# Moving two weight stores and two raw weight loads ahead of the first output weights' store, and stores of sums ahead of stores of weights

## The chip, the core and the metric

The kernel runs on one core of a Trainium2 chip. The time is the device time of one execution in microseconds; a result is the median of several. The engines are TensorE (PE, matrix products), VectorE (DVE), ScalarE (ACT), GpSimd (POOL) and SyncE (SP), which here does no arithmetic and only issues transfers (DMAs) between the chip's main memory (DRAM) and the on-chip memory (SBUF). ACT issues a few DMAs of its own. Each engine takes its instructions in a fixed order, and one that has to wait holds up everything behind it on that engine.

## The reference

```python
# attention in chunks of 64 positions: q, k, v are (8, 8, 576, 64)
scores = scale * np.matmul(q_c, k_c.transpose(0, 1, 2, 4, 3))
attn = np.exp(scores - np.max(scores, axis=-1, keepdims=True))
attn = attn / (np.sum(attn, axis=-1, keepdims=True) + 1e-09)
out = np.matmul(attn, v_c)
# gated feed-forward: x is (4608, 512), w_gate and w_val (512, 1536), w_out (1536, 512)
g = x @ w_gate
silu = g * (1.0 / (1.0 + np.exp(-g)))
val = x @ w_val
return (silu * val @ w_out).astype(np.float32)
```

The three weight matrices come as 64-bit floats, q, k and v as 32-bit ones.

## The kernel before

The 4608 tokens are cut into nine blocks of 512, and the 1536 hidden units into twelve groups f of 128. The first two blocks, `a0` and `a1`, go through the groups together, one step for each f, and the weights are prepared on the way; later blocks read the prepared weights back from DRAM. This case is about that opening, the first 116 us.

A product that must be close to 32-bit precision is done as three passes: each factor is split into an upper half (a rounded copy, made by ACT) and a lower half (the rest, made by DVE). One product of a block with a group's gate or value weights is 12 matmuls of 128x512.

These weights pass through the opening:

- **Raw up-weights**, `Up(f).load` (line 109): gate and value columns of group f as 64-bit words, a load of 1 MB. Below they are called raw f. ACT (`scale`, line 80, and `below`, line 87) and DVE (`shift`, line 83, and `join`, line 90) turn them into 32-bit floats `t`; `upper` (ACT, line 124) and `lower` (DVE, line 130) split those into the tile `w` of group f.
- **Stores of weights**, `save_w(f)` (line 197): the split tile w f goes to DRAM, 1 MB, for later blocks.
- **Sums**, `Quarters(f)`: DVE makes sums and differences of quarters of `t` (lines 148 to 150) in the tile `ts`; `upper` (ACT, line 162) and `lower` (DVE, line 165) split them into the tile `th`, and `save` (line 170) stores the two halves, 0.5 MB each. Below that pair of stores is t f. Through step 6 there is one `th` buffer: the halves for group f + 1 can only be written when t f has landed in DRAM.
- **Raw output weights**, `Out(f).load` (line 236): 1 MB for two groups, so only an even f issues a load (wo 2, wo 4); for an odd f it issues nothing. `out_weights(f)` (line 63 on DVE is its last part) splits them, and `save_o(f)` (line 489) stores o f, 0.5 MB.
- **put_off** (line 577): ACT issues a store of 0.25 MB in each step, the hidden values of `a1`.

One step f, for f from 1 to 5 (the loop of line 808), puts five pieces of 12 matmuls on PE: the gate of `a0`, its value, the projection of `a0` for the step before (lines 538 to 540), the gate of `a1`, its value. The products (line 475) share two PSUM buffers (`ps_gv`): a value of `a0` can start when DVE has taken the value of `a1` of the step before (`times`, line 519), a value of `a1` when DVE has taken that of `a0`, and a gate when ACT has taken the gate before it (`silu`, line 512). In between DVE and ACT prepare group f + 1, and from step 2 on they also make sums of the blocks' inputs (lines 773 to 786, tiles `sums` and `x`), which are put where w 0 to w 3 and raw 3 were. From step 6 (line 857) each product of the pair is replaced by seven smaller ones.

PE, ACT, DVE and, through the opening, SP run in the order in which the code is written (`manual_schedule`). So the order of SP's DMAs is that of the calls: in the opening's text, and then at the head of each step (lines 810 to 816) and, for f up to 2, line 823. Which buffer a tile takes is set by its tag: raw 3 lies in `w8`, where the first attention stage kept its turned exponents, wo 2 where `a0` kept its scores.

The line numbers of the profile of before are those of this listing.

Of the kernel before, what the change touches and what calls it, by code (L numbers as in the profile page):

```python
# [33 lines left out]
def attn_then_gated_ffn(ctx: ExitStack, tc: tile.TileContext, qk, v, wgv, wo, out):  # L34
# [19 lines left out]
    def keep_warm(n):  # L54

        ps = ps_gv.tile([P, P], F32, name="unread", tag="ps_gv")
        for _ in range(n):
            nc.tensor.transpose(ps, ident, ident)
# [78 lines left out]
    class Quarters:  # L137
# [12 lines left out]
            engine.tensor_tensor(out=s[:, 3], in0=t[:, 1], in1=s[:, 2], op=ALU.subtract)  # L150

        def place(self):
            if self.f >= SEVEN and self.f % 2:
                if not odd_t:
                    odd_t.extend(xs.tile([P, 4 * Q], F32R, name="th", tag=tag) for tag in ("xh0", "xl0"))
                return list(odd_t)
            both = const.tile([P, 2, 4 * Q], F32R, name="th", tag="th")
            return [both[:, 0], both[:, 1]]
# [14 lines left out]
    SEVEN, EARLY = 6, 4  # L173
# [21 lines left out]
    def save_w(f):  # L195
        kept_w[f] = store.tile([P, 2, 4 * Q], F32, name=f"w{f}")
        nc.sync.dma_start(out=kept_w[f], in_=w_both[f].bitcast(F32))
# [279 lines left out]
    def out_weights(f):  # L477
        both = wp.tile([P, 2, DM], F32R, name="both", tag="wo")
        split(wo_raw[f], both[:, 0], both[:, 1])
        if f % 2 == 0:  # L480
            o = store.tile([P, 2, 2, DM], F32, name=f"o{f}")
            kept_o[f], kept_o[f + 1], two_o[f // 2] = o[:, 0], o[:, 1], o
        out_now[f] = both
        return both[:, 0], both[:, 1]
# [3 lines left out]
    def save_o(f):  # L488
        nc.sync.dma_start(out=kept_o[f], in_=out_now[f].bitcast(F32))
# [17 lines left out]
    def gate(a, f):  # L507
        return silu(product(a, f, 0))

    def silu(pg):  # L510
        h = hp.tile([P, N], F32, name="h")
        nc.scalar.activation(h, pg, AF.Silu, scale=2.0 ** -8)
        return h

    def value(a, f):
        return product(a, f, 1)

    def times(h, pv):
        nc.vector.scalar_tensor_tensor(out=h, in0=pv, scalar=2.0 ** -8, in1=h, op0=ALU.mult, op1=ALU.mult)  # L519
# [6 lines left out]
    def parts(a, f, h):  # L526
        hh = hp.tile([P, N], F32R, name="hh")
        hl = hp.tile([P, N], F32R, name="hl")
        split(h, hh, hl)
        return a, f, hh, hl  # L530
# [27 lines left out]
    def lag(parts, wo_f):  # L558

        if pending:  # L560
            project(*pending.pop())
        if parts is not None:
            pending.append((parts, wo_f))
# [5 lines left out]
    up, down = [Up(f) for f in range(NF)], [Out(f) for f in range(NF)]  # L569
    waiting = []  # L570

    def put_off(h):
        f = len(waiting)
        if f % 2 == 0:
            kept_h.append(store.tile([P, 2, N], F32, name=f"h{f}"))
        waiting.append(kept_h[-1][:, f % 2])
        nc.scalar.dma_start(out=waiting[f], in_=h)
# [141 lines left out]
    for do in opening.split():  # L719
        if do[0] == ".":  # L720
            keep_warm(int(do[1:]))
        elif do[0] in "gvw":
            getattr(weights[do[:-1]], steps[do[-1]])()
        elif do[0] in "GV":
            if do[0] not in products:
                products[do[0]] = Product(a0, 0, "GV".index(do[0]))
            products[do[0]].add((int(do[3]), int(do[4])))
        elif do[0] == "e":
            a0.exchange(v0[int(do[1])][:, 1], values[int(do[1])][1], nc.scalar.copy)
        elif do == "H0":  # L730
            h0 = silu(products["G"].ps)
        elif do == "Q0":
            times(h0, products["V"].ps)
        else:
            b, i = int(do[1]), int(do[2])
            pairs = do[0] in "STCUL"
            getattr(couples[b, i // 2 if pairs else i], do[0])(i if pairs else int(do[3:] or 0))
    w = up[1]
    pg, pv = Product(a1, 0, 0), Product(a1, 0, 1)
    pg.add((0, 1), (1, 1), (0, 2), (1, 2), (2, 1), (3, 1), (2, 2), (3, 2))  # L740
# [5 lines left out]
    pv.add((0, 0), (1, 0), (2, 1), (3, 1), (2, 2), (3, 2), (2, 0), (3, 0))  # L746
    pv1 = pv.ps
    w.lower()
    o.shift()
    o.join()  # L750
    quarters = Quarters(1)
# [1 line left out]
    p0 = parts(a0, 0, h0)  # L753
    wo_f = out_weights(0)
    lag(p0, wo_f)
    down[1].load()
    down[1].scale()
    quarters.upper()

# [47 lines left out]

    for f in range(1, SEVEN):
        w, o = up[f + 1], down[f]
        save_o(f - 1)  # L810
        up[f + 2].load()
        if f <= EARLY:
            save_w(f - 1)
        if f > 2:
            quarters.save()
        down[f + 1].load()
        ahead.get(f, lambda: None)()
        h0 = gate(a0, f)
        times(h1, pv1)
        put_off(h1)  # L820
        if f <= 2:
            quarters.lower()
            quarters.save()
        quarters = Quarters(f + 1)
        w.shift()
        w.below()
        pv0 = value(a0, f)
        o.shift()
        o.below()
        beside.get(f, lambda: None)()  # L830
        w.join()
        w.upper()
        times(h0, pv0)
        within.get(f, lambda: None)()
        p0 = parts(a0, f, h0)
        w.lower()
        o.join()
        quarters.sums(w.t)
        up[f + 2].scale()
        wo_f = out_weights(f)  # L840
        lag(p0, wo_f)
        h1 = gate(a1, f)
        quarters.upper()
        down[f + 1].scale()
        if f > 1:
            quarters.lower()
        pv1 = value(a1, f)
# [402 lines left out]
    for i in range(NF):  # L1250
        f = (i + EARLY) % NF
# [67 lines left out]
```

## Time and profile before

| | us |
|---|---|
| median of 3 runs | 904.18 (902.27 to 905.06) |
| the profiled execution | 903.28 |
| its span | 901.5 |
| PE busy in the span | 885.2 (98%) |
| DVE busy | 545.6 (61%) |
| ACT busy | 386.1 (43%) |

The span runs from the first to the last recorded instruction; the remaining 1.78 us of the execution lie around it. A row of the timeline reads: start in the span, length, engine, line and operation, what it writes and from what, the shape, how many, and in square brackets how long the engine stood idle before it and what ended that. "SPq" and "ACTq" are issues of DMAs; the length there is that of the issue, not of the transfer. 223.25 MB are moved in all, at a mean of 248 GB/s. The granted clock of TensorE is 1.00 throughout.

### The profile page before, as it was taken

To read this page: it belongs to the slowest core of one execution; us is meant where nothing else is said; L and a number is where in the kernel's file an instruction comes from. 1 tells how busy PE (TensorE), PEld (TensorE's weight loads), DVE (VectorE), ACT (ScalarE), POOL (GpSimd) and SP (SyncE) were. 2 spreads that over 40 slices of the span, in tenths; PEclk is the share of its full clock that TensorE was granted. 3 is DMA by queue.
4 is the path that set the end of the run, shared out by engine and by line. 5 is a ranking of instruction groups with operands and counts; after the bars stand their busy time and mean duration, and the time that the engine had idled before them with its cause. 6 is when DMAs were issued, how large, how long until landed. Compare 5 with 4: busy or idle time off the path is not lost.

```text
span 901.5 us, 14751 instructions
## 1 busy us (share of the span) xinstructions
PE 885.2 (98%) x6047; PEld 731.7 (81%) x6047; DVE 545.6 (61%) x834; ACT 386.1 (43%) x587; POOL 17.1 (2%) x18
## 2 busy tenths in 40 slices
PE   7998999999999999999999999999999999999998
PEld 6776788878888888888888888888888888888886
DVE  5869899853787655775763646776645533333332
ACT  4846677653514335324233445234334432223232
POOL 1200000000021000000000000000000000000000
PEclk9999999999999999999999999999999999999999
DMA  9297977799898657755586857665667565556651
GB/s 358 112 377 264 323 291 274 291 315 349 271 359 286 253 198 258 258 213 180 217 294 236 333 185 282 233 228 195 220 245 242 212 237 201 196 220 233 234 187 47
DMA packets 73170, 223.25 MB, mean 248 GB/s; under 512 B 30736, under 2 KB 30992, under 8 KB 58896
## 3 DMA queue, kind: packets, MB, share of 16 engines
q1 hardware_dynamic: 71664, 219.70, 67.3%
q10 hardware_dynamic: 1440, 2.62, 0.8%
q8 instruction: 47, 0.77, 0.3%
q14 instruction: 19, 0.16, 0.0%
HBM read 178.78 MB, written 43.52 MB: 247 GB/s over the span
## 4 chain that ended last, share of the span: by engine, by line
PE 90%; DMA 4%; DVE 4%; ACT 1%; issue 1%; POOL 0%; SPq 0%; ACTq 0%
PE ps_a L857 25%; PE ps_gv L857 19%; PE ps_o L538 11%; PE ps_o L539 10%; PE ps_o L540 10%; PE ps_gv L475 10%; DMA t<-th 3%; PE ps_a L287 2%; PE ps_a L365 1%; DMA qk_t<-in_qk 1%; ACT th L162 0%; DVE sums L776 0%; PE ps_a L451 0%; PE ps_a L465 0%; DVE th L165 0%
## 5 line engine op out<-in xcount | busy, mean ns | idle before, releaser
L857 PE MATMUL ps_a<-x,factors 128*128 128x512 f32 x864 | 219.3, 389 | 0.0
L857 PEld LDWEIGHTS ps_a<-x,factors 128*128 128x128 f32 x864 | 162.2, 188 | 33.7
L857 PE MATMUL ps_gv<-x,factors 128*128 128x512 f32 x648 | 164.5, 389 | 0.0
L857 PEld LDWEIGHTS ps_gv<-x,factors 128*128 128x128 f32 x648 | 121.7, 188 | 25.2
L538 PE MATMUL ps_o<-both,hl 128*128 128x512 f32 x336 | 132.3, 394 | 0.2 <-DVE hl L63 0.2
L539 PE MATMUL ps_o<-both,hh 128*128 128x512 f32 x336 | 131.0, 390 | 0.0
L540 PE MATMUL ps_o<-both,hh 128*128 128x512 f32 x336 | 130.9, 389 | 0.0
L475 PE MATMUL ps_gv<-xh,w 128*128 128x512 f32 x384 | 117.0, 390 | 0.2 <-ACT xh L614 0.2
L63 DVE TENSOR_TENSOR hl<-h,hh 128x512 fp32r<-128x512 f32 x98 | 67.6, 690 | 61.7 <-ACT hh L62 61.5
L62 ACT CAST hh<-h 128x512 fp32r<-128x512 f32 x98 | 60.4, 617 | 96.1 <-PE ps_o L540 51.3
L861 DVE TENSOR_TENSOR h<-h,ps_gv 128x512 f32<-128x512 f32 x42 | 28.8, 686 | 105.6 <-PE ps_gv L857 105.4
L352 DVE STREAM_TRANSPOSE turned<-s_sb 32x256 f32<-32x256 f32 x192 | 83.7, 436 | 2.7
L475 PEld LDWEIGHTS ps_gv<-xh,w 128*128 128x128 f32 x384 | 72.0, 188 | 15.7 <-issue 0.7
L519 DVE SCALAR_TENSOR_TENSOR h<-v,h 128x512 f32<-128x512 f32 x84 | 58.1, 692 | 37.7 <-ACT h L1153 33.0
L475 PE MATMUL ps_gv<-xl,w 128*128 128x512 f32 x192 | 74.0, 395 | 5.3 <-DVE h L519 2.9
L538 PEld LDWEIGHTS ps_o<-both,hl 128*128 128x128 f32 x336 | 63.1, 188 | 14.1 <-DVE hl L63 0.7
L540 PEld LDWEIGHTS ps_o<-both,hh 128*128 128x128 f32 x336 | 63.1, 188 | 13.2
L539 PEld LDWEIGHTS ps_o<-both,hh 128*128 128x128 f32 x336 | 63.1, 188 | 12.7
L1153 ACT ACTIVATE h<-ps_a 128x512 f32<-128x512 f32 x36 | 21.5, 599 | 112.2 <-PE ps_a L857 112.2
L861 DVE TENSOR_TENSOR v<-v,ps_a 128x512 f32<-128x512 f32 x42 | 28.8, 687 | 41.1 <-PE ps_a L857 36.4
L475 PEld LDWEIGHTS ps_gv<-xl,w 128*128 128x128 f32 x192 | 36.0, 188 | 14.2 <-DVE h L519 4.5
L1139 ACT ACTIVATE h<-h 128x512 f32<-128x512 f32 x36 | 22.8, 632 | 53.0 <-DVE h L861 52.9
(132 smaller groups left out, 1007.4 us busy)
## 6 DMA issues: line engine op xcount, KB each, us to landing
factors<-w SPq DMA_DIRECT2D x36, 1024.0 KB, 4.8
factors<-t SPq DMA_DIRECT2D x36, 1024.0 KB, 6.0
both<-o SPq DMA_DIRECT2D x70, 512.0 KB, 6.3
w<-w SPq DMA_DIRECT2D x16, 1024.0 KB, 9.7
t<-th SPq DMA_DIRECT2D x24, 512.0 KB, 5.8
two<-o SPq DMA_DIRECT2D x12, 1024.0 KB, 5.0
raw<-in_wgv SPq DMA_DIRECT2D x11, 1024.0 KB, 8.2
qk_t<-in_qk SPq DMA_DIRECT2D x10, 1024.0 KB, 8.4
```

The lines of the kernel that those rows point to most:

```text
L62: nc.scalar.copy(out=hi, in_=src)
L63: (engine or nc.vector).tensor_tensor(out=lo, in0=src, in1=hi.bitcast(F32), op=ALU.subtract)
L352: nc.vector.transpose(out=self.turned[to:to + 32, p:p + 2, j, :, 32 * (i % 2):32 * (i % 2) + 32], in_=src[32 * i:32 * i + 32, :, o // 2, 3 ...
L475: nc.tensor.matmul(ps, w, x, start=first and (k, i) == which[0], stop=last and (k, i) == which[-1])
L519: nc.vector.scalar_tensor_tensor(out=h, in0=pv, scalar=2.0 ** -8, in1=h, op0=ALU.mult, op1=ALU.mult)
L538: nc.tensor.matmul(o, hl[:, ts], woh, start=f == a.steps[0], stop=False)
L539: nc.tensor.matmul(o, hh[:, ts], wol, start=False, stop=False)
L540: nc.tensor.matmul(o, hh[:, ts], woh, start=False, stop=f == a.steps[1])
L857: nc.tensor.matmul(ps, w[u][:, k], x[i][v][:, k], start=first and k == 0 and n == 0, stop=k == NK // 2 - 1 and n == 2, skip_group_check=True)
L861: nc.vector.tensor_tensor(out=t, in0=t, in1=ps, op=ALU.add)
L1139: nc.scalar.activation(h, h, AF.Silu, scale=2.0 ** -8)
L1153: nc.scalar.activation(h2, ps1, AF.Silu, scale=2.0 ** -8)
```

## The change

No instruction is added or removed on any engine: SP has 310 rows in the order of both versions, and PE, DVE, ACT and POOL run the same instructions in the same order. What moves is SP's DMAs.

```diff
@@ class Quarters
         def place(self):
-            if self.f >= SEVEN and self.f % 2:
+            if (self.f - SEVEN) % 2 and self.f > SEVEN:
@@ after the opening's list of steps
+    save_w(0)
+    up[3].load()
+    down[1].load()
+    down[2].load()
     w = up[1]
...
     w.lower()
+    save_w(1)
     o.shift()
...
     lag(p0, wo_f)
-    down[1].load()
     down[1].scale()
@@ the loop over steps
     for f in range(1, SEVEN):
         w, o = up[f + 1], down[f]
+        if f > 1:
+            up[f + 2].load()
         save_o(f - 1)
-        up[f + 2].load()
-        if f <= EARLY:
-            save_w(f - 1)
         if f > 2:
             quarters.save()
-        down[f + 1].load()
+            if f <= EARLY:
+                save_w(f - 1)
+        if f > 1:
+            down[f + 1].load()
         ahead.get(f, lambda: None)()
```

`SEVEN` is 6 and `EARLY` is 4. The new condition in `place` picks the same groups as the old one (7, 9 and 11).

The first place is SP's queue from the end of the opening's loads to the stores of step 2. `raw<-in_wgv` is a raw up-weight (raw 3, then raw 4), `raw<-in_wo` the raw output weights (the first row wo 0, the second wo 2), `w_` a store of weights (w 0, then w 1), `o_` a store of output weights (o 0, then o 1), `t_` the two stores of sums (t 1, then t 2). Before:

```order
L236 DMA raw<-in_wo 128x2x512
L489 DMA o_707<-both 128x1024
L109 DMA raw<-in_wgv 128x1024
L197 DMA w_716<-w 128x2048
L236 DMA raw<-in_wo 128x2x512
L170 DMA t_739<-th 128x1024 x2
L489 DMA o_707<-both 128x1024
L109 DMA raw<-in_wgv 128x1024
L197 DMA w_830<-w 128x2048
L170 DMA t_850<-th 128x1024 x2
```

and after the change:

```order
L236 DMA raw<-in_wo 128x2x512
L197 DMA w_661<-w 128x2048
L109 DMA raw<-in_wgv 128x1024
L236 DMA raw<-in_wo 128x2x512
L197 DMA w_700<-w 128x2048
L489 DMA o_715<-both 128x1024
L170 DMA t_741<-th 128x1024 x2
L109 DMA raw<-in_wgv 128x1024
L489 DMA o_715<-both 128x1024
L170 DMA t_850<-th 128x1024 x2
```

w 0, raw 3, wo 2 and w 1 now stand ahead of o 0, behind which all of them stood; between o 0 and t 1 nothing is left, where raw 3, w 0 and wo 2 were; raw 4 now stands ahead of o 1.

The second place is SP's queue in steps 3 and 4, from step 3's first row on (raw 5, o 2, w 2, t 3, wo 4, then raw 6, o 3, w 3, t 4 are what is issued). Before:

```order
L489 DMA o_894<-both 128x1024
L109 DMA raw<-in_wgv 128x1024
L197 DMA w_944<-w 128x2048
L170 DMA t_946<-th 128x1024 x2
L236 DMA raw<-in_wo 128x2x512
L489 DMA o_894<-both 128x1024
L109 DMA raw<-in_wgv 128x1024
L197 DMA w_1060<-w 128x2048
L170 DMA t_1062<-th 128x1024 x2
```

and after the change:

```order
L109 DMA raw<-in_wgv 128x1024
L489 DMA o_894<-both 128x1024
L170 DMA t_944<-th 128x1024 x2
L197 DMA w_947<-w 128x2048
L236 DMA raw<-in_wo 128x2x512
L109 DMA raw<-in_wgv 128x1024
L489 DMA o_894<-both 128x1024
L170 DMA t_1060<-th 128x1024 x2
L197 DMA w_1063<-w 128x2048
```

Each step's raw load now stands ahead of its store of output weights, and each store of sums ahead of the store of weights.

## The prediction

> **What bounds the kernel now.** PE is busy for 885.2 of 901.5 us, so only its gaps can be won. I first read PE's waits, then its timeline from 44 to 120 us, the only stretch in which SP's order changes and PE still has gaps. The waits, with their total, count and longest:
>
> ```profile
> PE ps_gv L475 <- DVE h L519: 2.9, 4, 1.2
> PE ps_gv L475 <- ACT h L512: 1.7, 1, 1.7
> ```
>
> The timeline places all five, and gives PE's pace:
>
> ```profile
> 47.83 0.39 PE L538 MATMUL ps_o<-both,hl 128*128 128x512 f32 x1
> ...
> 58.25 0.62 PE L475 MATMUL ps_gv<-xh,w 128*128 128x512 f32 x2
> ...
> 61.42 0.39 PE L538 MATMUL ps_o<-both,hl 128*128 128x512 f32 x1
> ...
> 68.19 0.50 PE L475 MATMUL ps_gv<-xl,w 128*128 128x512 f32 x1 [1.17 <-DVE h L519]
> ...
> 72.87 0.50 PE L475 MATMUL ps_gv<-xl,w 128*128 128x512 f32 x1 [1.66 <-ACT h L512]
> ...
> 75.27 0.61 PE L475 MATMUL ps_gv<-xh,w 128*128 128x512 f32 x2
> 76.17 0.50 PE L475 MATMUL ps_gv<-xl,w 128*128 128x512 f32 x1 [0.29 <-DVE h L519]
> ...
> 90.31 0.50 PE L475 MATMUL ps_gv<-xl,w 128*128 128x512 f32 x1 [0.23 <-DVE h L519]
> ...
> 105.37 0.50 PE L475 MATMUL ps_gv<-xl,w 128*128 128x512 f32 x1 [1.17 <-DVE h L519]
> ...
> 116.39 0.39 PE L857 MATMUL ps_a<-xl,w 128*128 128x512 f32 x1
> ```
>
> From 47.83 to 61.42, without a gap, 60 matmuls take 13.59 us, 0.2265 each. From 61.42 to step 6 there are 216 more, 48.92 us: step 6 would begin at 110.34, and begins at 116.39. So the five gaps cost **6.05 us**: 4.52 recorded, and some 0.3 each for emptying and refilling the array (the first matmul takes 0.50 instead of 0.39). That is the ceiling.
>
> Why are DVE and ACT late there? ACT's timeline answers:
>
> ```profile
> 60.88 1.05 ACT L162 CAST th<-ts 128x1024 fp32r<-128x1024 f32 x1 [6.47 <-DMA t<-th]
> ...
> 62.89 1.14 ACT L87 ACTIVATE t<-raw 128x1024 int32<-128x1024 uint32 x1
> ...
> 72.22 0.59 ACT L512 ACTIVATE h<-ps_gv 128x512 f32<-128x512 f32 x1
> ...
> 75.98 0.60 ACT L512 ACTIVATE h<-ps_gv 128x512 f32<-128x512 f32 x1 [0.20 <-PE ps_gv L475]
> ...
> 76.52 1.16 ACT L87 ACTIVATE t<-raw 128x1024 int32<-128x1024 uint32 x1
> ...
> 102.41 1.05 ACT L162 CAST th<-ts 128x1024 fp32r<-128x1024 f32 x1 [2.95 <-DMA t<-th]
> ```
>
> Twice ACT waits for the store of sums to leave `th`, and DVE waits behind it. DVE's rows that PE's gaps hang on:
>
> ```profile
> 64.05 2.36 DVE L773 TENSOR_TENSOR sums<-xh,xl 128x1024 f32<-128x1024 f32 x2
> ...
> 67.45 0.69 DVE L519 SCALAR_TENSOR_TENSOR h<-ps_gv,h 128x512 f32<-128x512 f32 x1
> ...
> 75.44 0.68 DVE L519 SCALAR_TENSOR_TENSOR h<-ps_gv,h 128x512 f32<-128x512 f32 x1
> ...
> 89.57 0.68 DVE L519 SCALAR_TENSOR_TENSOR h<-ps_gv,h 128x512 f32<-128x512 f32 x1
> ...
> 104.64 0.68 DVE L519 SCALAR_TENSOR_TENSOR h<-ps_gv,h 128x512 f32<-128x512 f32 x1
> ```
>
> **The first wait.** The five issues from o 0 to t 1 (first and last row), and the landing of t 1's halves from SP's line 170:
>
> ```profile
> 44.33 0.34 SPq L489 DMA_DIRECT2D o<-both  x1
> ...
> 46.53 1.38 SPq L170 DMA_DIRECT2D t<-th  x2
> ```
>
> ```profile
> DMA to landing us min/median/max: 12.1/12.9/13.7
> ```
>
> o 0, raw 3, w 0, wo 2 and t 1 are 4.5 MB (0.5 and four of 1), done at 60.88, 16.55 us after the first issue: 3.7 us per MB. With the change, w 0 issues after its lower half, raw 3 and wo 2 when PE has read the old content, w 1 after its lower half:
>
> ```profile
> 35.78 0.86 PE L465 MATMUL ps_a<-pT,v_t 64*64 64x64 f32 x43
> ```
>
> ```profile
> 24.70 0.77 DVE L222 TENSOR_TENSOR w<-t,w 128x512 fp32r<-128x512 f32 x1
> ...
> 39.18 1.22 DVE L130 TENSOR_TENSOR w<-t,w 128x1024 fp32r<-128x1024 f32 x1
> ...
> 44.81 1.22 DVE L165 TENSOR_TENSOR th<-ts,th 128x1024 fp32r<-128x1024 f32 x1
> ```
>
> That is 25.5, 36.7 and 40.4 us, in a stretch where the queues are empty:
>
> ```profile
> 36.00:44.00 8.00, 7.84 (x75) 6.47 (x65) 7.35 (x13) 6.87 (x12) 0.00 (x0) 1.00 0.01 3
> ```
>
> (the last two numbers are the DMA engines' share and GB/s). raw 3, wo 2 and w 1, 3 MB from 36.7, are through at 47.8; o 0 and t 1, 1.5 MB more, at 53.4. ACT wanted `th` from 60.88 - 6.47 = 54.41. The wait goes, with 1 us to spare, and 3 more before it would be felt, as now follows.
>
> **What is late next.** The 6.5 us don't all arrive. ACT's `below` (62.89) stands behind the silu of `a0`'s gate, which waits for PE: in step 3 the gate's last pair ends at 75.88, and `below` starts at 76.52, 0.64 later. In step 2 the pair ends at 58.87, so `below` starts at 59.51, **3.38 us** earlier. The sums at 64.05 wait for its end, and what follows on DVE and ACT up to 76 us moves by the same 3.38, since both then run with waits for each other alone. Against PE's ungapped times (61.42 plus 24, 36, 48 matmuls, then 13.59 a step):
>
> - 68.19: the value of `a1` is due at 66.86; `times` at 67.45 comes at 64.07. Gone.
> - 72.87: the gate is due at 69.57; the silu at 72.22 comes at 68.84 and frees the buffer 0.65 later, at 69.49. Gone, by 0.1 us.
> - 76.17: due at 72.29; `times` at 75.44 comes at 72.06 and PE starts 0.73 later, 72.79. Stays, 0.50 late, and 0.12 for the slower first matmul.
> - 90.31: DVE needs 14.13 us from one `times` (75.44) to the next (89.57), more than PE's 13.59. It comes at 86.19, PE at 86.93 against a due 86.50. Stays; PE is now 86.93 + 0.12 - 85.88 = 1.17 behind the ungapped time.
> - 105.37: without the second wait `th` is written at 102.41 - 2.95 - 3.38 = 96.08, and `times`, 2.23 behind that, at 98.31; done at 99.0, PE wants it at 100.64. Gone, with 1.6 us to spare.
>
> Sum: 6.05 - 1.17 = **4.9 us**.
>
> **The second wait.** It takes t 4 landing by 96.08. SP's rows, and the landings of t 3 and wo 4 (lines 170 and 236):
>
> ```profile
> 73.76 0.32 SPq L489 DMA_DIRECT2D o<-both  x1
> ...
> 75.42 1.40 SPq L170 DMA_DIRECT2D t<-th  x2
> 78.27 0.38 SPq L236 DMA_DIRECT2D raw<-in_wo  x1
> ...
> 89.59 1.04 SPq L170 DMA_DIRECT2D t<-th  x2
> ```
>
> ```profile
> DMA to landing us min/median/max: 10.8/11.0/11.1
> ```
>
> ```profile
> DMA to landing us min/median/max: 11.0/11.0/11.0
> ```
>
> From o 2 (73.76) to t 4 (landed by 102.4, where ACT's wait ends) nine SP entries are 8 MB, plus two of ACT's 0.25: 28.6 us for 8.5 MB. The change takes raw 5 out ahead (it issues after t 2) and puts w 3 behind: 6.5 MB, 21.9 us from an o 2 that comes at 73.76 - 3.38 = 70.4: landed at 92.3, 3.8 us early. That counts on transfers finishing in the queue's order, as here: t 3, issued at 75.42 and about 76, is in by 87; wo 4 behind it at 89.3.
>
> The Trainium skill's page "DMA: Bandwidth & Descriptors" (Queues, rings and completion order) says that descriptors are consumed in ring order but completion is not in order of issue. Were t 4 to share the engines with w 3 behind it, being ahead would gain nothing; the landings above speak for ring order, and the sum goes by them. By that rule the time is the second rival's.
>
> **The rest costs nothing, for these reasons.** `place` picks the same groups. No byte is added. The early transfers run beside DVE: its 128x1024 subtraction takes 1.22 us at 39.18, with idle DMA, and 1.22 at 44.81, with busy ones; bound 0 either way. w 0's store, at 25.5, may start beside raw 2, which ACT takes without a wait at
>
> ```profile
> 30.96 1.13 ACT L80 ACTIVATE t<-raw 128x1024 f32<-128x1024 f32 x1
> ```
>
> In the queue's order that costs 0, shared at most w 0's own 3.7 us; I take 0, by the order of t 3 and wo 4. What SP's queue holds up: behind raw 3, which waits for PE until 36.7, stand wo 2, w 1, o 0 and t 1, and o 0 and t 1 are not ready before 44.3 and 46.0. Behind the raw loads of steps 2 to 5 stand the stores, but their buffers were read a step before. w 2 and w 3 go later than t: ACT writes `x` over w 2 at
>
> ```profile
> 92.89 1.04 ACT L782 CAST x<-sums 128x1024 fp32r<-128x1024 f32 x1
> ```
>
> less 3.4, 89.5; w 2 issues at about 73 and the four stores of w landed within 11.7 us:
>
> ```profile
> DMA to landing us min/median/max: 9.6/10.3/11.7
> ```
>
> so by 84.7, 4.8 us early. After step 6 PE has no gap up to 190 us, so the 4.9 us carry through to the end.
>
> **The rivals.**
>
> - All five gaps vanish, if the sums' chain in steps 2 and 3 is shorter than I copy it: 6.05, 897.2 us. Against it: 14.13 per step on DVE with one wait of half a us.
> - t 4 still lands late. If completion is shared, w 3's 1 MB (3.4 us) and raw 7's count too: 92.3 + 6.8 = 99.1, `th` 3.0 late, less the 1.6 to spare: 1.4 and the refill, gain 3.4: 899.9 us. For it: the engines' rows are full here, with 8.5 MB in 28.6 us; against it the order t 3, wo 4.
> - PE gains little: t 1 lands no earlier than 60.88 - 1, because raw 3, wo 2 and w 1 issue late. The step begins to lose at 57.4 (60.67 for the sums, less 3.3 for both halves and two shifts). Then DVE moves by 1, and the gain is near 1 to 2: 902 us.
> - Slower: w 2's store, now behind t 3, holds `x`. It decides from 16 us after its issue; 1.6 are to spare on DVE, 4.9 are won, so net loss starts at 22.5 us, and 26 us give 906.8. No store took half of 22.5.
>
> **The numbers.** The profiled execution took 903.28, its span 901.5; 903.28 - 4.9 = 898.4. It lies 0.9 below the median of the runs, 904.18, on whose scale the forecast is 899.3. I give 898.8, between them. Chances: forecast 0.57 (897.4 to 900.2), all gone 0.10, t 4 late 0.18, little gain 0.11, slower 0.04. A range from 896.7 to 901.4 leaves out little gain and slower and some spread. 0.3% is 2.7 us, about what a measurement of this kernel tells from no change; faster by more takes a time below 901.5: 0.57 + 0.10 + 0.18 less 0.03 for their tails, 0.82. Within 0.3%: 0.14. Slower: 0.04.
>
> **What would show it.** ACT's wait at line 162 for `t` gone in step 1 and step 4; `below` of step 2 at about 59.5; PE's gaps reduced to two of 0.3 to 0.4 us near 72.8 and 86.9; the first matmul of line 857 at about 111.5. It is wrong if the gaps at 68 or 72 remain (the 0.1 us), if t 4's wait stays, or if a wait for `w` appears at line 782.

## The result, and the profile after

| | before | changed |
|---|---|---|
| median of 4 runs, us | 903.98 (902.27 to 905.06) | 897.48 (897.17 to 897.97) |
| the profiled execution | 903.28 | 897.36 |
| its span | 901.5 | 895.6 |

The ratio is 0.993, with a 95% interval of 0.9913 to 0.9948: 6.5 us faster by the medians, 5.9 by the two profiled executions. The forecast gain was 4.9, taken from the profiled execution.

PE's timeline of the changed kernel holds the same three marks as before (the projections of steps 1 and 2, the first matmul of step 6). Lines from the opening on are four to six higher than before: 857 is 863, 773 is 777.

```profile
47.62 0.39 PE L538 MATMUL ps_o<-both,hl 128*128 128x512 f32 x1
...
61.22 0.39 PE L538 MATMUL ps_o<-both,hl 128*128 128x512 f32 x1
...
110.22 0.39 PE L863 MATMUL ps_a<-xl,w 128*128 128x512 f32 x1
```

From 61.22 to 110.22 are 49.00 us; the ungapped time is 48.92, and before it took 54.97. All five gaps are gone, also the two that the prediction kept: 5.97 us. PE's waits say the same. Both rows at line 475 of before, 2.9 and 1.7 us, are missing, and what is left on line 475 is

```profile
PE ps_gv L475 <- ACT s_sb L368: 0.8, 1, 0.8
...
PE ps_gv L475 <- ACT xh L614: 0.2, 1, 0.2
```

which lie outside the stretch from 44 to 110 us. ACT's writing of `th`, which waited 6.47 and 2.95 us for stores:

```profile
54.02 1.05 ACT L162 CAST th<-ts 128x1024 fp32r<-128x1024 f32 x1 [0.16 <-DMA t<-th]
...
94.66 1.04 ACT L162 CAST th<-ts 128x1024 fp32r<-128x1024 f32 x1
```

The first wait: SP's rows of the opening (w 0, raw 3, wo 2, w 1, o 0, t 1), the time to landing of t 1's halves, and the rows of DVE that follow:

```profile
25.27 0.34 SPq L197 DMA_DIRECT2D w<-w  x1
36.52 0.34 SPq L109 DMA_DIRECT2D raw<-in_wgv  x1
36.95 1.16 SPq L236 DMA_DIRECT2D raw<-in_wo  x1
40.21 0.33 SPq L197 DMA_DIRECT2D w<-w  x1
44.11 0.33 SPq L489 DMA_DIRECT2D o<-both  x1
44.52 1.63 SPq L170 DMA_DIRECT2D t<-th  x2
```

```profile
DMA to landing us min/median/max: 8.1/8.1/8.2
```

```profile
56.03 0.69 DVE L519 SCALAR_TENSOR_TENSOR h<-ps_gv,h 128x512 f32<-128x512 f32 x1 [1.84 <-ACT wo L80]
56.64 1.22 DVE L165 TENSOR_TENSOR th<-ts,th 128x1024 fp32r<-128x1024 f32 x1
```

The second wait: SP's queue in steps 3 and 4, and the time to landing of t 4's halves, first in the kernel before, then in the changed one:

```profile
69.00 0.32 SPq L489 DMA_DIRECT2D o<-both  x1
69.52 1.58 SPq L170 DMA_DIRECT2D t<-th  x2
71.16 0.62 SPq L197 DMA_DIRECT2D w<-w  x1
74.58 0.38 SPq L236 DMA_DIRECT2D raw<-in_wo  x1
75.02 1.13 SPq L109 DMA_DIRECT2D raw<-in_wgv  x1
83.19 0.33 SPq L489 DMA_DIRECT2D o<-both  x1
83.71 1.58 SPq L170 DMA_DIRECT2D t<-th  x2
```

```profile
DMA to landing us min/median/max: 11.5/11.8/12.2
```

```profile
DMA to landing us min/median/max: 3.4/3.5/3.6
```

Between raw 6 at 75.02 and o 3 at 83.19 SP issues nothing, and raw 6 lands 8.8 us after its issue, at 83.8. So t 4 finds the queue almost empty but for o 3, and lands 3.5 us after its issue instead of 11.8.

ACT's `below` in step 2, and DVE's rows in step 2 and behind it, where the prediction had put the two sums together:

```profile
59.25 1.13 ACT L87 ACTIVATE t<-raw 128x1024 int32<-128x1024 uint32 x1
```

```profile
58.71 1.22 DVE L777 TENSOR_TENSOR sums<-xh,xl 128x1024 f32<-128x1024 f32 x1
60.41 1.23 DVE L777 TENSOR_TENSOR sums<-xh,xl 128x1024 f32<-128x1024 f32 x1 [0.48 <-ACT t L87]
...
70.67 0.68 DVE L519 SCALAR_TENSOR_TENSOR h<-ps_gv,h 128x512 f32<-128x512 f32 x1
...
84.86 0.68 DVE L519 SCALAR_TENSOR_TENSOR h<-ps_gv,h 128x512 f32<-128x512 f32 x1
```

Only the second sum waits for ACT's reading of raw 3 (line 87). `times` comes at 70.67, where 72.06 was forecast.

### The profile page after: what moved, and what is told of

Same layout as the page of the kernel before. It is cut to its first block, busy times and chain, and to the rows that moved or that the text cites. A ratio compares the mean times of both kernels' runs of the same rounds, so it can differ in the third digit from the quotient of the medians.

```text
span 895.6 us, 14752 instructions
## 1 busy us (share of the span) xinstructions
PE 884.2 (99%) x6047; PEld 732.2 (82%) x6047; DVE 546.6 (61%) x834; ACT 386.6 (43%) x587; POOL 17.1 (2%) x18
## 4 chain that ended last, share of the span: by engine, by line
PE 94%; DVE 2%; DMA 2%; POOL 0%; ACT 0%; issue 0%; SPq 0%; DVEq 0%; POOLq 0%
PE ps_a L863 26%; PE ps_gv L863 19%; PE ps_gv L475 13%; PE ps_o L538 11%; PE ps_o L540 11%; PE ps_o L539 11%; PE ps_a L287 2%; DMA v_t<-in_v 2%; DVE turned L352 1%; PE ps_a L365 1%; DMA qk_t<-in_qk 1%; PE ps_a L465 0%; POOL v_t L408 0%; DVE h L519 0%; PE ps_a L451 0%
## 5 line engine op out<-in xcount | busy, mean ns | idle before, releaser
L867 DVE TENSOR_TENSOR v<-v,ps_gv 128x512 f32<-128x512 f32 x42 | 28.9, 688 | 24.5 <-PE ps_gv L863 24.2
```

What stands on the lines that cost most here:

```text
L867: nc.vector.tensor_tensor(out=t, in0=t, in1=ps, op=ALU.add)
```

## The experiments

The diffs are against the changed kernel. The column "stretch" is the time on PE from the projection of step 1 (first row at line 538) to the first matmul of step 6, 276 matmuls, 62.51 us without gaps: it leaves out the opening's start, which differs by up to 0.8 us from profile to profile. The four from "opening's part only" to "raw behind o" ran on one chip beside the kernel before (904.36), the last four on another beside the kernel before (903.53); the last of these is the changed kernel once more.

| kernel | median us | stretch, from and to | stretch | gaps in it |
|---|---|---|---|---|
| before (first profile) | 903.98 | 47.83 to 116.39 | 68.56 | 4.52 in five |
| changed (first profile) | 897.48 | 47.62 to 110.22 | 62.60 | none |
| opening's part only | 898.96 | 47.96 to 112.23 | 64.27 | 1.40 in one |
| steps' part only | 901.75 | 48.33 to 114.93 | 66.60 | 2.83 in four |
| w ahead of t | 897.67 | 47.81 to 110.41 | 62.60 | none |
| raw behind o | 898.29 | 47.73 to 110.31 | 62.58 | none |
| sums swapped | 898.90 | 48.02 to 111.73 | 63.71 | 0.54 in two |
| one more store | 897.96 | 47.90 to 110.47 | 62.57 | none |
| two more stores | 900.82 | 48.24 to 113.25 | 65.01 | 1.50 in three |
| changed, again | 897.38 | 47.52 to 110.08 | 62.56 | none |

**The opening's part alone.**

```diff
 for f in range(1, SEVEN):
-        if f > 1:
-            up[f + 2].load()
         save_o(f - 1)
+        if f > 1:
+            up[f + 2].load()
+        if 2 < f <= EARLY:
+            save_w(f - 1)
         if f > 2:
             quarters.save()
-            if f <= EARLY:
-                save_w(f - 1)
```

> Keeps the opening's part of the change (w 0, raw 3, wo 2, w 1 ahead of o 0) and puts steps 2 to 5 back to the old order (o, raw, w, t). Theory: the first wait for t stays away, so PE's gaps at 68 to 90 us stay away; t 4 again has o 3, raw 6 and w 3 ahead of it, lands some 12 us after its issue as before, and ACT waits some 2.4 us for it in step 4, which leaves one gap of 0.6 to 0.9 us on PE near 99 us: about 0.9 us over the changed kernel. Rival (the steps' part is worth nothing once the opening is emptied): no wait for t 4, and the changed kernel's time.

The rows of ACT and PE, and t 4's landing:

```profile
98.25 1.05 ACT L162 CAST th<-ts 128x1024 fp32r<-128x1024 f32 x1 [3.18 <-DMA t<-th]
```

```profile
101.22 0.50 PE L475 MATMUL ps_gv<-xl,w 128*128 128x512 f32 x1 [1.40 <-DVE h L519]
```

```profile
DMA to landing us min/median/max: 11.5/12.0/12.4
```

The theory holds: t 4 lands after 12 us as before, ACT waits, one gap is back. It is 1.40 us wide, not 0.6 to 0.9, since ACT waited 3.18 us instead of 2.4. The stretch is 1.7 us longer than the changed kernel's, the median 1.3 above that of the kernel with w ahead of t, which ran beside it and has no gap; 0.9 was expected.

**The steps' part alone.**

```diff
-    save_w(0)
-    up[3].load()
-    down[1].load()
-    down[2].load()
     w = up[1]
...
     w.lower()
-    save_w(1)
...
     lag(p0, wo_f)
+    down[1].load()
...
         save_o(f - 1)
-        if f > 2:
+        if f <= 2:
+            if f == 1:
+                up[3].load()
+            save_w(f - 1)
+            down[f + 1].load()
+        else:
             quarters.save()
             if f <= EARLY:
                 save_w(f - 1)
-        if f > 1:
             down[f + 1].load()
```

> Keeps the part of the change in the steps (raw first, t ahead of w) and puts the opening back to the old order (o 0, raw 3, w 0, wo 2, then t 1). Theory: t 1 lands at about 61 as before, ACT waits 6 us for it, and PE's gaps at 68, 73, 76 and 90 us come back, 4.6 us together; the gap at 105 us stays away. So about 4.6 us over the changed kernel, 1.4 under the one before. Rival (t 1 is not what PE's gaps hang on): most of the gain stays.

ACT, and PE with all its gaps between 44 and 110 us:

```profile
60.85 1.05 ACT L162 CAST th<-ts 128x1024 fp32r<-128x1024 f32 x1 [6.06 <-DMA t<-th]
```

```profile
68.15 0.50 PE L475 MATMUL ps_gv<-xl,w 128*128 128x512 f32 x1 [0.62 <-DVE h L519]
...
72.83 0.50 PE L475 MATMUL ps_gv<-xl,w 128*128 128x512 f32 x1 [1.66 <-ACT h L512]
...
76.13 0.50 PE L475 MATMUL ps_gv<-xl,w 128*128 128x512 f32 x1 [0.29 <-DVE h L519]
...
90.32 0.50 PE L475 MATMUL ps_gv<-xl,w 128*128 128x512 f32 x1 [0.26 <-DVE h L519]
```

The first four gaps are back, the fifth isn't. The stretch is 4.0 us longer than the changed kernel's, and the medians differ by 4.3 (by 4.1 from the kernel with w ahead of t, which ran beside it); it is 2.6 us under the kernel before on the same chip, where 1.4 was expected. So the change is two cures: the opening's part does away with the first four gaps, the steps' part with the fifth. The stretch shortens by 4.29 us with the one (68.56 - 64.27), by 1.96 with the other (68.56 - 66.60) and by 5.96 with both. The two single gains add up to 0.29 more than the gain of both. That is a balance of two differences: the first gap is 0.55 narrower here than before (0.62 against 1.17), since PE came to it 0.5 us later while `th` was written at the same time, and the gap that the opening's part leaves is 0.23 wider than before (1.40 against 1.17).

**w ahead of t again, and raw behind o again.**

```diff
         if f > 2:
-            quarters.save()
             if f <= EARLY:
                 save_w(f - 1)
+            quarters.save()
```

> The changed kernel with the store of weights put back ahead of the store of sums in steps 3 and 4; raw loads stay first. Theory: t 4 lands later by w 3's own transfer, 2.5 to 3.4 us, so some 6 to 7 us after its issue instead of 3.5, at about 91; ACT wants it at 94.7, so there is no gap and no cost. Rival (completion is shared among transfers in flight, so the place in the queue does not matter): t 4 lands 3.5 us after its issue as in the changed kernel.

```diff
-        if f > 1:
-            up[f + 2].load()
         save_o(f - 1)
+        if f > 1:
+            up[f + 2].load()
```

> The changed kernel with each raw load of steps 2 to 5 put back behind the store of output weights; stores of sums stay ahead of those of weights. Theory: raw 6 stands ahead of t 4 again, which lands 6 to 7 us after its issue; no wait on ACT, no cost. Rival (raw's place is what cured step 4): ACT waits for t 4 and PE has a gap near 99 us, 0.9 us.

t 4's landing in the one and in the other, and ACT's write of `th` in the other:

```profile
DMA to landing us min/median/max: 6.1/7.3/8.5
```

```profile
DMA to landing us min/median/max: 9.5/9.9/10.3
```

```profile
95.47 1.05 ACT L162 CAST th<-ts 128x1024 fp32r<-128x1024 f32 x1 [0.61 <-DVE both L63]
```

With w 3 ahead of it t 4 takes 7.3 us instead of 3.5: its place in the queue does matter, and the rival is refuted. Raw 6 ahead of it costs more than was expected, 9.9 instead of 6 to 7; a half issued at 85.1 that takes 10.3 us is in at 95.4, and ACT writes `th` at 95.47, 0.6 us after it was free. (The profile names line 63 on DVE as what ended that wait; that instruction writes `both`, not `th` or `ts`, so the landing is the likelier cause.) Neither costs PE a gap, nor the stretch a tenth. Each of the two orders is enough by itself; the kernel before had neither, and both transfers together made the 12 us.

**The sums swapped.** The prediction's failed step, put to the test.

```diff
     def begin():
         raw.append(Raw())
-        raw[0].whole(a1, 0, S4)
         raw[0].whole(a1, 1, S1)
+        raw[0].whole(a1, 0, S4)
```

> The changed kernel, but in step 2 DVE makes the sum that lies in raw 3's place first and the other second; nothing else differs. Theory: only the sum in raw 3's place has to wait for ACT's second reading of raw 3 (line 87, ending at 60.4); the prediction took both to wait, and was 1.2 us too late on DVE. Put first, it makes both wait, as the prediction had it: DVE comes 1.2 us later from there on, PE gets two gaps of 0.3 to 0.5 us near 72.6 and 86.8, and the time is about 1.2 us over the changed kernel. Rival (the prediction's two gaps failed for another reason, such as a faster step on DVE): no gap and the changed kernel's time.

DVE's sums and the two `times` that they delay, then PE:

```profile
60.79 2.36 DVE L777 TENSOR_TENSOR sums<-xh,xl 128x1024 f32<-128x1024 f32 x2 [1.60 <-ACT t L87]
...
72.19 0.68 DVE L519 SCALAR_TENSOR_TENSOR h<-ps_gv,h 128x512 f32<-128x512 f32 x1
...
86.37 0.68 DVE L519 SCALAR_TENSOR_TENSOR h<-ps_gv,h 128x512 f32<-128x512 f32 x1
```

```profile
72.93 0.50 PE L475 MATMUL ps_gv<-xl,w 128*128 128x512 f32 x1 [0.27 <-DVE h L519]
...
87.11 0.50 PE L475 MATMUL ps_gv<-xl,w 128*128 128x512 f32 x1 [0.27 <-DVE h L519]
```

With both sums behind ACT, the two gaps that the prediction saw are there: forecast at 72.79 and 86.93, found at 72.93 and 87.11. They are 0.27 us wide, just under the 0.3 to 0.5 expected; with some 0.3 us more for each, as in the kernel before, they make the stretch 1.15 us longer (63.71 against 62.56), as expected, and the median is 1.5 above that of the changed kernel on the same chip.

**One and two more stores ahead of t 1.** The diff is that of the second kernel; the first has `range(1)`.

```diff
     save_w(1)
+    for i in range(2):
+        spare = store.tile([P, 2, 4 * Q], F32, name=f"spare{i}")
+        nc.sync.dma_start(out=spare, in_=w_both[1].bitcast(F32))
```

> The changed kernel with one more 1 MB store (w 1 once more, to a tile that nobody reads) between w 1 and o 0. Theory: t 1 lands 2.5 to 3.7 us later, at 56.5 to 57.7 instead of 54.0; the first sum of step 2 loses its place in front of ACT's reading of raw 3, and DVE is 0.5 to 1.6 us later: 0.5 to 1.7 us over the changed kernel. Rival (3 us to spare, as predicted): no cost.

> The changed kernel with two more 1 MB stores between w 1 and o 0. Theory: t 1 lands 5 to 7.4 us later, at 59 to 61.4, ACT waits 5 to 7 us for it, and PE's gaps of the kernel before come back: 3.5 to 5.3 us over the changed kernel, with every us of t 1 beyond the first mega-byte costing about one. Rival: the gaps have another cause, and the time stays within 1 us of the changed kernel.

ACT's write of `th` in step 1, with one and with two:

```profile
55.79 1.05 ACT L162 CAST th<-ts 128x1024 fp32r<-128x1024 f32 x1 [1.59 <-DMA t<-th]
```

```profile
59.15 1.05 ACT L162 CAST th<-ts 128x1024 fp32r<-128x1024 f32 x1 [4.61 <-DMA t<-th]
```

t 1's time to landing in the changed kernel (second profile), with one and with two:

```profile
DMA to landing us min/median/max: 7.3/7.4/7.6
```

```profile
DMA to landing us min/median/max: 9.6/9.8/10.0
```

```profile
DMA to landing us min/median/max: 12.6/12.8/13.0
```

One store more costs nothing that the runs can tell: no gap, a stretch of 62.57, and 897.96 against 897.38 with overlapping ranges. That expectation missed: `th` written at 55.8 is still early enough. Two cost 2.45 us in the stretch and 3.4 in the median (just under the 3.5 to 5.3 expected), with `th` 3.4 us later than with one; of the first four gaps three are back, near 71, 74 and 89 us, and the one at 68 is not. DVE's rows, with one store and with two:

```profile
56.33 0.69 DVE L519 SCALAR_TENSOR_TENSOR h<-ps_gv,h 128x512 f32<-128x512 f32 x1 [1.86 <-PE ps_gv L475]
56.94 1.22 DVE L165 TENSOR_TENSOR th<-ts,th 128x1024 fp32r<-128x1024 f32 x1
...
62.91 0.69 DVE L519 SCALAR_TENSOR_TENSOR h<-ps_gv,h 128x512 f32<-128x512 f32 x1
```

```profile
56.67 0.69 DVE L519 SCALAR_TENSOR_TENSOR h<-ps_gv,h 128x512 f32<-128x512 f32 x1 [1.86 <-PE ps_gv L475]
60.23 1.23 DVE L165 TENSOR_TENSOR th<-ts,th 128x1024 fp32r<-128x1024 f32 x1 [2.87 <-ACT th L162]
...
65.72 0.69 DVE L519 SCALAR_TENSOR_TENSOR h<-ps_gv,h 128x512 f32<-128x512 f32 x1
```

With one, DVE is held by PE until 56.33 and takes `th` (ready at 56.84) right behind; with two it stands idle for it. So a later landing of t 1 costs nothing as long as `th` is written by 55.8. The profile with two began the stretch 0.34 us later than that with one; less this, `th` is written 3.02 us later, the next `times` comes 2.47 later, and the stretch is 2.44 longer. So 0.55 of the 3.02 were still free, the rest cost PE about one us for each, and the turning point is near 56.3, an estimate from these two profiles. The prediction had put it at 57.4.

**The changed kernel again.**

> The changed kernel itself, on the chip of the three runs above, to compare them with: 897.5 us, no gap on PE between 44 and 110 us.

897.38 us, no gap, a stretch of 62.56.

## Why the prediction was right, and where it was off

The measured 897.48 lies inside the range (896.7 to 901.4), and the mechanism is the one forecast: two waits of ACT for the store of sums. The likeliest case, 898.8, was not what happened; the rival "all five gaps vanish" (897.2, a chance of 0.10) was. The range took that rival in, so that the time lies inside it says nothing for the two gaps that were forecast to stay: on them the prediction was wrong. Step by step:

- **The ceiling**, 6.05 us: 5.96 came out of the stretch. The opening, which the change does not shorten by any step of the prediction, ended 0.2 earlier in this profile, so step 6 began 6.17 earlier (110.22; the forecast was about 111.5), and some 0.25 is lost again behind it. PE's waits there have one row that the kernel before lacks, 0.2 us at line 287 for DVE's line 519. Both are within what the profiles differ by.
- **The first wait**: forecast to go with 1 us to spare at 53.4. ACT's wait for t 1 ended at 54.02, with 0.16 us of wait left; in the second profile of the changed kernel ACT wrote `th` at 53.66 without a wait. So ACT had next to nothing to spare. What followed on DVE covered it: with `times` at 56.03 ahead of it, DVE could not have used `th` before 56.64. "3 more before it would be felt" was too much: 1.8 are shown to be free (one more store), 5.1 are not, and the estimate of 56.3 leaves some 2.
- **What is late next**: `below` in step 2 was forecast at 59.51 and came at 59.25. The step that failed is the sentence behind it, "the sums at 64.05 wait for its end, and what follows ... moves by the same 3.38". The row at 64.05 stands for two instructions (x2, 2.36 us). Only the sum in raw 3's place waits for ACT's reading; the other lies in another buffer, and in the profile before it began beside the end of that reading by chance, because DVE's own queue had only just come to it. In the changed kernel it runs ahead, in time that the prediction counted as waiting. `times` moved by 4.77 us (75.44 to 70.67), 0.2 of it from the opening, instead of 3.38; the difference is about one sum, 1.2 us.
- **The gaps at 76 and 90**, forecast to stay at 1.17 us together: with `times` done at 71.35 and 85.54, PE, due at 72.08 and 85.67, was not held. In the second there was 0.1 us to spare: DVE's 14.13 us from one `times` to the next, more than PE's 13.59, was read rightly (14.19 here). The swapped sums brought both gaps back.
- **The gaps at 68, 72 and 105**: gone, as forecast.
- **The second wait**: right in direction, too cautious in size. t 4 was to land at 92.3, behind 6.5 MB from an o 2 at 70.4; its last half was issued at 85.0 and landed by 88.6. o 2 came 1.4 us sooner, at 69.00, since DVE did, and the rest went in 19.6 us instead of 21.9. One of the two stores of ACT that the sum counts, 0.25 MB, was issued only behind t 4; why the others took less time per MB than in the kernel before, no run shows.
- **The rival with shared completion** (899.9): the runs speak against it. In all ten profiles SP's transfers between 20 and 112 us landed in the order in which they were issued, and t 4's time to landing followed what stood ahead of it in the queue, 3.5, 7.3, 9.9 and 12.0 us, in four kernels that move the same bytes. The Trainium skill's page "DMA: Bandwidth & Descriptors" (Queues, rings and completion order) says that completion is not first in, first out for an issuing engine, and gives as its case a later transfer on one DMA engine beside an earlier one on sixteen. That t 4 would share its time with w 3 was the prediction's own step from there; for these transfers on SP's queue the measured order is that of issue. The place in the queue doesn't settle everything, though. With the same transfers ahead of it, t 1 took 8.1, 7.4, 8.2 and 8.2 us to land in four profiles, and 6.6 in the two kernels that don't have raw 4 directly behind it (opening's part only, raw behind o). No run tests whether raw 4 is the cause.
- **The edits costed at nothing** show no cost. ACT's reading of raw 2, beside which w 0's store may run, has no wait at 30.75 (line 80), and ACT's copies over w 2 and w 3 (line 786) show no wait for a store, at 88.06 and at 101.64. The sentence "no store took half of 22.5" was wrong as it stood, since the halves of t 1 took 12.1 to 13.7 us in the kernel before and a store of w up to 11.7; but none came near 22.5, and w 2 and w 3 take 6.3 and 7.3 in the changed kernel:

```profile
88.06 1.04 ACT L786 CAST x<-sums 128x1024 fp32r<-128x1024 f32 x1
...
101.64 1.04 ACT L786 CAST x<-sums 128x1024 fp32r<-128x1024 f32 x1
```

What stays open: why the profile of the changed kernel moved 5.9 us and the medians 6.5. The kernel before ranged over 2.8 us in four runs, so the difference is within what its runs differ by.

## What to carry to other kernels

A row that stands for several instructions must be opened before a wait is put on it: here one of two instructions was waiting, and that one mattered for a fifth of the gain. Where a buffer's release hangs on a store, order the queue by who waits for each transfer, and move what nobody waits for, and what could have gone earlier, out from in front of it; a queue that is full in one burst may stand empty just before. And a wait that goes is worth only as much as the next thing on the same engines leaves of it, so write down what each engine would wait for then.

## What was not expected of the hardware

Transfers through this queue had no one price per MB. With one more 1 MB store in front of it t 1 took 9.8 us to land and with two 12.8, so the second store added 3.0. The first added 1.7 to 2.4, by which of the two profiles of the changed kernel it is measured from (8.1 and 7.4): a single profile's landing is uncertain by most of a us. The burst of the kernel before had taken 3.7 us per MB, its start included. The 0.5 MB halves of t 4 in the changed kernel, with little but o 3 ahead of them, landed 3.4 to 3.6 us after their issue.
